# A planned order of tasks against a fixed list of all tasks, in a fused attention and feed-forward kernel

## The chip, the cores and the metric

The kernel runs on one core of one Trainium2 chip. Its time is the device time of one execution in microseconds, from the chip's own counters. The number that is predicted is the median of several executions.

A core has five engines that work side by side, each with a queue of its own that it works through in the order written: TensorE (PE, matrix products), VectorE (DVE), ScalarE (ACT), GpSimd (POOL) and SyncE (SP). Here POOL and SP mostly issue transfers. An engine waits at the head of its queue until the semaphores of that instruction allow it; what stands behind it waits too.

## The reference

```python
# attention, batch 8, heads 8, seq 576, head_dim 64
scores = scale * np.matmul(q, k.transpose(0, 1, 3, 2))
thresh = np.max(scores, axis=-1, keepdims=True) - tau
scores = np.where(scores >= thresh, scores, -1000000000.0)
scores = scores - np.max(scores, axis=-1, keepdims=True)
attn = np.exp(scores)
attn = attn / (np.sum(attn, axis=-1, keepdims=True) + 1e-09)
out = np.matmul(attn, v)
# (B,H,S,D) -> (4608, 512), then the feed-forward layer
h = x @ w_in                                # 512 -> 2048
g = h * (1.0 / (1.0 + np.exp(-1.702 * h)))
y = g @ w_out                               # 2048 -> 512
```

All in float32. The two weights are loaded once and rewritten on the chip, the feed-forward rows are taken in 18 blocks of 256 tokens.

## The kernel before

**Attention.** Two heads make a pair; there are 32 pairs, 0 to 31. A pair's scores come in nine groups of 64 keys: `scores` (L818) computes one group on TensorE as four 64x64 tiles side by side, `keep` (L835, ACT) copies it out of PSUM, `in_groups` (L858, DVE) takes maxima. After the row maximum is spread, `sub` (L940, DVE) or an accumulating transfer (`add_mb`, L933, POOL queue) takes it off, `mask` (L947) and `exps` (L951) run on ACT, and `values` (L962, TensorE, again 64x64 tiles) multiplies by v. Three PSUM places ("psA") hold scores on their way; a group of scores needs one, and `keep` frees it. From pair 6 on, the values of one pair and the scores of the next are written as one **run**: values of two groups, two groups of scores, and so on, fourteen pieces in turn. I write V12.1 for part 1 of the values of pair 12, S13.2 for group 2 of the scores of pair 13. Such a run uses TensorE in four small tiles; the feed-forward products use it whole (128x128).

**Feed-forward.** Blocks 0 and 1 use plain products (`mm1_0`, L1159, then `tanh`, L1116, on ACT and `gelu_0`, L1165, on DVE). Later blocks use seven products of half blocks in place of eight (`product1`, L1223, and `product4`, L1396, for the first layer; `product`, L1704, for the second). I write P0.0 for the first task of `product` of block 0. The last six blocks, after the last pair, use two levels of this (`product2`, L1551; `product3`, L1660); DVE and ACT do the additions and copies around them. Before the second layer can start, the 32 pieces of the weights are converted on ACT and DVE as they land (`cv_power`, `cv_power2`, `cv_whole`, `cv_end`, L746 to L771) and summed (`t_whole`, L1289).

**The order.** All work is first noted as 4767 tasks by `task(...)`, each with an engine, a cost, a rank and the tasks it comes after. `run_in_order` then plays a clock forward: at each moment an engine that is free takes, of the tasks that are ready and find their buffers free, the one with the lowest rank, and emits its instructions. A list of ranks, `PLACES`, one number for each task, sets the choice. Transfers are tasks of two movers ("DMS", "DMW") with a rate. `follows` ties the pieces of a run: once TensorE has begun a run, `held_for` keeps it from taking anything else until the next piece is ready:

```python
for rank, i in queue if engine in MOVERS else sorted(queue):
    if engine == "PE" and held_for not in (None, i):
        continue
```

and `need` lets a run begin only with all three psA places free. Forty tiny products (`stay_warm`, L1770) are tasks of the lowest rank, used while TensorE has nothing else, up to about 37 us. What is emitted is a plain program: the planner is gone when the chip runs it, and each engine's instructions stand in the order in which the planner took them.

Of the kernel before, what the change touches and what calls it, by code (L numbers as in the profile page):

```python
# [17 lines left out]
ALU = mybir.AluOpType  # L18
# [14 lines left out]
def kernel(  # L33
# [40 lines left out]
    NKT = NK // 2  # L74
# [179 lines left out]
    ALIKE = ("sub", "keep", "x_sum", "x_sum0", "x_sum3", "read", "in_groups", "cv_low", "cv_round", "place_x")  # L254
# [28 lines left out]
    def transfer(by, time, a, kind=0, give=(), lag=1.7):  # L283
# [6 lines left out]
    PLACES = """  # L290
# [2562 lines left out]
```

## Time and profile before

| what | us |
|---|---|
| median of 3 executions (1219.2 to 1220.19) | 1219.4 |
| the profiled execution's own time | 1218.41 |
| its span, first to last instruction | 1216.6 |
| PE busy in the span | 1194.1 |
| DVE busy | 1067.2 |
| ACT busy | 794.0 |
| POOL busy | 130.8 |

PE is busy 98% of the span, but that is an average over stages. A busy PE can also be one that runs tiny products to fill time, or one whose clock was halved. The profile is read by stretches of the span: which engine has no idle time in each, and what it is that PE waits for.

### The profile page before, as it was taken

The page shows a single profiled execution, that of the slowest core. Times are in us where ns is not written, and L with a number is a line of the kernel's source. Part 1 is how long each engine was busy: PE and PEld are TensorE (multiplying, and loading weights), DVE is VectorE, ACT ScalarE, POOL GpSimd, SP SyncE. Part 2 cuts the span into 40 slices and gives each one's busy share as a digit, 9 for nine tenths or more (in the row PEclk, how much of TensorE's full clock was granted, in tenths as well). Part 3 has the DMA queues.
Part 4 walks back from the last instruction along what each step waited for, and adds up shares of the span by engine and source line. Part 5 has one row for each costly group of instructions (what it writes and reads, how often), then busy time and mean ns, then how long its engine had stood idle before and what let it go on. Part 6 is the DMA issues. An engine that isn't in the chain of part 4 may idle for free.

```text
span 1216.6 us, 26169 instructions
## 1 busy us (share of the span) xinstructions
PE 1194.1 (98%) x10560; PEld 979.7 (81%) x10560; DVE 1067.2 (88%) x1622; ACT 794.0 (65%) x1183; POOL 130.8 (11%) x176
## 2 busy tenths in 40 slices
PE   8899999999999999999999999999999999999998
PEld 6556777788877777777777777777778999999998
DVE  6998998989989888999889867997896799899797
ACT  7999986888686779668876659667872340340340
POOL 0112232110001110011100110021100000000000
PEclk9999999999999999999999999999999999999999
DMA  8866769787555664567635743567623544544442
GB/s 263 225 137 157 189 146 178 138 157 198 132 131 122 143 164 93 133 145 183 142 74 123 175 108 79 123 138 179 166 59 123 183 137 142 165 135 144 141 139 94
DMA packets 220616, 176.55 MB, mean 145 GB/s; under 512 B 148752, under 2 KB 165776, under 8 KB 220368
## 3 DMA queue, kind: packets, MB, share of 16 engines
q1 hardware_dynamic: 197776, 125.42, 37.9%
q0 software_dynamic: 22032, 49.17, 20.3%
q8 instruction: 83, 1.36, 0.5%
q10 hardware_dynamic: 688, 0.30, 0.1%
q14 instruction: 37, 0.30, 0.1%
HBM read 119.53 MB, written 25.84 MB: 119 GB/s over the span
## 4 chain that ended last, share of the span: by engine, by line
PE 79%; ACT 14%; DVE 3%; issue 1%; DMA 1%; ACTq 0%; DVEq 0%
PE ops L1704 24%; PE hps L1396 9%; PE pv L962 9%; PE ps L818 9%; PE ps L1396 7%; PE ops L1660 6%; PE hps L1551 5%; PE ps L1660 4%; PE ps L1551 4%; ACT arena L835 3%; ACT arena L947 3%; ACT arena L951 3%; PE hps L1223 2%; DVE arena L1568 1%; PE ps L1223 1%
## 5 line engine op out<-in xcount | busy, mean ns | idle before, releaser
L858 DVE TRANSPOSE_TENSOR_REDUCE part<-arena 128x36 f32<-128x1152 f32 (+1 forms) x250 | 296.7, 1213 | 25.1 <-ACT arena L835 18.5
L835 ACT COPY arena<-ps 128x576 f32<-128x576 f32 x288 | 172.3, 646 | 52.3 <-PE ps L818 49.4
L947 ACT ACTIVATE arena<-arena 128x1152 f32<-128x1152 f32 (+1 forms) x160 | 167.8, 1064 | 55.2 <-DVE arena L940 53.7
L951 ACT ACTIVATE arena<-arena,shift 128x1152 f32<-128x1152 f32 (+1 forms) x160 | 183.8, 1160 | 2.4
L818 PE MATMUL ps<-arena 64*64 64x288 f32 x2304 | 173.1, 408 | 10.8 <-ACT arena L835 7.3
L1704 PE MATMUL ops<-w_out,arena 128*128 128x256 f32 x768 | 173.9, 381 | 2.7 <-DVE arena L1165 2.7
L1704 PEld LDWEIGHTS ops<-w_out,arena 128*128 128x128 f32 x768 | 144.5, 190 | 28.1 <-issue 4.4
L962 PE MATMUL pv<-arena 64*64 64x288 f32 x2176 | 159.4, 405 | 0.0
L818 PEld LDWEIGHTS ps<-arena 64*64 64x64 f32 x2304 | 81.0, 132 | 74.6 <-ACT arena L835 32.1
L940 DVE TENSOR_TENSOR arena<-arena 128x1152 f32<-128x1152 f32 (+1 forms) x100 | 130.3, 1339 | 0.8
L962 PEld LDWEIGHTS pv<-arena 64*64 64x64 f32 x2176 | 80.5, 133 | 52.4 <-issue 5.6
L1565 ACT COPY arena<-hps 128x512 f32<-128x512 f32 x66 | 38.6, 585 | 114.8 <-PE hps L1551 114.8
L1704 PE MATMUL ops<-arena 128*128 128x256 f32 x464 | 104.3, 379 | 0.0
L933 POOL DMA_DIRECT2D arena<-arena x50 | 54.3, 1321 | 422.0 <-DVE arena L898 246.2
L1704 PEld LDWEIGHTS ops<-arena 128*128 128x128 f32 x464 | 88.0, 190 | 12.8 <-issue 0.4
L848 DVE TRANSPOSE_TENSOR_REDUCE part<-arena 128x72 f32<-128x2304 f32 x25 | 64.3, 2573 | 14.7 <-ACT arena L951 14.5
L1396 PE MATMUL hps<-xT,w_in 128*128 128x256 f32 x256 | 59.0, 381 | 0.0
L1396 PEld LDWEIGHTS hps<-xT,w_in 128*128 128x128 f32 x256 | 48.1, 190 | 8.9 <-issue 2.2
L878 ACT ACTIVATE other<-red,gap 32x18 f32<-32x18 f32 x100 | 30.7, 307 | 36.9 <-DVE red L867 35.8
L1159 PE MATMUL hps<-xT,w_in 128*128 128x256 f32 x232 | 53.0, 389 | 0.0
L1437 ACT COPY arena<-hps 128x512 f32<-128x512 f32 x64 | 37.0, 578 | 24.0 <-PE hps L1396 23.9
L1568 DVE TENSOR_TENSOR arena<-ps,arena 128x512 f32<-128x512 f32 x63 | 42.8, 686 | 10.0 <-ACT arena L1565 7.6
(224 smaller groups left out, 2045.2 us busy)
## 6 DMA issues: line engine op xcount, KB each, us to landing
arena<-in_v_dram SPq DMA_DIRECT2D x128, 144.0 KB
arena<-exu SPq DMA_DIRECT2D x63, 256.0 KB
arena<-ext SPq DMA_DIRECT2D x60, 256.0 KB
arena<-arena POOLq DMA_DIRECT2D x25, 576.0 KB, 6.1
arena<-wrow POOLq DMA_DIRECT2D x48, 256.0 KB, 4.6
arena<-in_k_dram SPq DMA_DIRECT2D x112, 72.0 KB
arena<-in_q_dram SPq DMA_DIRECT2D x112, 72.0 KB
arena<-arena POOLq DMA_DIRECT2D x25, 288.0 KB, 7.3
```

The source lines that it names most:

```text
L818: nc.tensor.matmul(ps[ts(c, KT), h, 0:SH], lhsT=mats[n, 1][ts(h, D), ts(j, KT)], rhs=mats[n, 0][ts(h, D), ts(c, SH)], start=True, stop=True,)
L835: nc.scalar.copy(out=sT[n, t][:, u], in_=pss.pop((n, j))[:, :, 0:SH])
L848: nc.vector.tensor_reduce(out=stats[n, ALU.add][:, t * 2 * QB : min(2 * t + 4, NK) * QB], in_=arena2[:, lo : mid + size].rearrange("p (c d ...
L858: nc.vector.tensor_reduce(out=stats[n, op][:, t * 2 * QB : min(2 * t + 2, NK) * QB], in_=sT[n, t].rearrange("p u h (g d) -> p (u h g) d", ...
L940: engine.tensor_tensor(out=s, in0=s, in1=mbs[n].unsqueeze(1).to_broadcast(list(s.shape)), op=ALU.add if n in BY_DMA or n in NEGATED else A ...
L947: nc.scalar.activation(out=s, in_=s, func=AF.Prelu, alpha=STEEP)
L951: nc.scalar.activation(out=s, in_=s, func=AF.Exp, scale=SCALE, bias=shift)
L962: nc.tensor.matmul(o[c][ts(h, D), 0:SH], lhsT=left(j, h)[ts(c, KT)], rhs=sT[n, t][ts(c, KT), u, h, :], start=(j == 0), stop=(j == NK - 1),)
L1396: nc.tensor.matmul(o[:, ts(j, BLK)], lhsT=left[:, c, ts(j, P)], rhs=right[:, c, :], start=(x in (P1, P2, P5) and j + c == 0), stop=(j + c ...
L1551: nc.tensor.matmul(o[:, ts(j, HT)], lhsT=left[:, ts(j, P)], rhs=right, start=(m in (P1, P2, P5) and j == 0), stop=(j == 3), skip_group_che ...
L1660: nc.tensor.matmul(banks3[pos, r][:, 0:HT], lhsT=left[:, j, :], rhs=right[:, j, :], start=(m in (P1, P2, P5) and j == 0), stop=(j == 3), s ...
L1704: nc.tensor.matmul(banks[blk][k][:, ts(o, HM)], lhsT=left[:, j, :], rhs=right[:, j, :], start=(j == 0), stop=(j == HF - 1),)
```

## The change

`PLACES`, the planner's clock, the movers' rates, `need` and `follows` are gone from the emission. In their place stands `ORDER`, a list of all 4767 task numbers, and the tasks are emitted in that order:

```diff
-    PLACES = """
+    ORDER = """
...
     def run_in_order():
-        for i, place in enumerate(PLACES):
-            tasks[i] = (*tasks[i][:2], int(place), *tasks[i][3:])
...
-                    if engine == "PE" and held_for not in (None, i):
-                        continue
...
-        assert started == len(tasks), (started, len(tasks))
+        assert len(ORDER) == len(tasks)
+        for i in map(int, ORDER):
+            x_free.extend(x_used.pop(key) for key in x_ends.get(i, ()) if key in x_used)
+            tasks[i][3](*tasks[i][4])
```

The costs given to `task(...)` are changed as well (for example 1.25 to 1.136 for `t_whole`); nothing reads them any more. The functions that emit instructions are the same, and so are the tasks. So the whole change is in the order of each engine's queue. Laid beside the order that the planner gave before, the list keeps this many tasks of each engine in their old relative order (the longest common sequence):

| engine | tasks | in the old order |
|---|---|---|
| PE | 1161 | 1042 |
| DVE | 1394 | 860 |
| ACT | 1055 | 808 |
| SP | 461 | 330 |
| POOL | 133 | 126 |

No task goes far: most are exchanged with neighbours. After 200 us the order on PE differs in few places until the last pair is done. These are the places on PE, with the tasks in question in brackets (the last line is one engine's neighbours on DVE and ACT):

```
block 0   before: mm1_0 13, [V5 whole], mm1_0 14, mm1_0 15, P0.0
          after:  mm1_0 13, mm1_0 14, mm1_0 15, [V5 whole], P0.0
run 6/7   before: V6.3 S7.6 S7.7 V6.4 S7.8 [P0.3 first half]
          after:  V6.3 S7.6 S7.7 [P0.3 first half] V6.4 S7.8
run 12/13 before: [P3.0 j0-3] V12.0 S13.0 S13.1 V12.1 S13.2 S13.3 V12.2 S13.4 ... S13.8 [P3.0 j4-6]
          after:  V12.0 S13.0 S13.1 V12.1 [P3.0 j0-3] S13.2 S13.3 V12.2 [P3.0 j4-6] S13.4 ... S13.8
run 19/20 before: [product4 6.0.3] V19.0 ... S20.3 V19.2 S20.4 ...
          after:  V19.0 ... S20.3 V19.2 [product4 6.0.3] S20.4 ...
run 25/26 before: V25.3 S26.6 S26.7 V25.4 S26.8 [P8.0 j7]
          after:  V25.3 [P8.0 j7] S26.6 S26.7 V25.4 S26.8
pair 31   before: [V31 whole], last product of block 10, first of block 11
          after:  last product of block 10, first of block 11, [V31 whole]
DVE       before: t_whole x4, sub 6.0, [sub 6.1, sub 6.2], gelu_0 14, gelu_0 15
          after:  t_whole x4, sub 6.0, gelu_0 14, gelu_0 15, ... [sub 6.1] ... [sub 6.2]
ACT, 19   before: exps 19.0, mask 19.1, mask 19.2, [keep4], exps 19.1, [keep4], exps 19.2, [keep4], mask 19.3, keep 20.0
          after:  exps 19.0, mask 19.1, exps 19.1, mask 19.2, exps 19.2, mask 19.3, keep 20.0, keep 20.1, [keep4]
```

In the first 40 us the list loads the second piece of the weights ahead of the q of pair 1, and the v of pair 0 five weight pieces later; the 40 `stay_warm` tasks are spread differently. In the last 265 us (`product2`, `product3`) many neighbours are exchanged on PE, DVE and ACT; the last four tasks of PE and the last two of DVE are the same.

More of the change, by code (lines that the diff above doesn't have):

```diff
@@ L253 @@
     AGAIN, COLD = {"DVE": 0.12, "ACT": 0.13}, 0.1
-    ALIKE = ("sub", "keep", "x_sum", "x_sum0", "x_sum3", "read", "in_groups", "cv_low", "cv_round", "place_x")
+    ALIKE = ("silu1", "silu4", "t_whole", "t_minus", "sub", "keep", "x_sum", "x_sum0", "x_sum3", "read", "in_groups", "cv_low", "cv_round", "place_x")
     ENTER = {True: 0.0, False: 0.22}
@@ L1829 @@
         ]
-        m = task("ACT", 0.75, rank, cv_power, i, after=[a] + over)
-        m = task("ACT", 0.56, rank, cv_power2, i, after=[m])
+        m = task("ACT", 0.667, rank, cv_power, i, after=[a] + over)
+        m = task("ACT", 0.62, rank, cv_power2, i, after=[m])
         if i in ROUND_BY_ACT:
@@ L1834 @@
         else:
-            a = task("DVE", 0.35, rank, cv_whole, i, after=[a])
-        ready_w.append(task("DVE", 0.61, rank, cv_end, i, after=[a, m], give=place))
+            a = task("DVE", 0.332, rank, cv_whole, i, after=[a])
+        ready_w.append(task("DVE", 0.602, rank, cv_end, i, after=[a, m], give=place))
     warm = task("ACT", 2.3, -2.0, first_act)
@@ L1891, in first_blocks @@
             a = task("ACT", 0.48, FIRST, tanh, j, after=ffn[-1:], take=("io",) + (("xT",) if j == 0 else ()))
-            gelus[j] = task("DVE", 0.59, FIRST, gelu_0, j, after=[a],
+            gelus[j] = task("DVE", 0.6, FIRST, gelu_0, j, after=[a],
                 give=("psM", "io"),
@@ L1899, in t_sum @@
                 for k in range(2):
-                    after = [task("DVE", 1.25, T_RANK, t_whole, x, k, after=after)]
+                    after = [task("DVE", 1.136, T_RANK, t_whole, x, k, after=after)]
                 t_ready.extend(after)
@@ L2309, in seven @@
         ):
-            last = task("ACT", 0.93, FIRST, silu1, f, h, after=after + [last])
+            last = task("ACT", 0.95, FIRST, silu1, f, h, after=after + [last])
             gs[f, h] = [last, last]
@@ L2387, in seven4 @@
                         keeps[x, y] = task(
[L2388 removed]
+                            "ACT", 0.466, FIRST, keep4, q, x, after=ffn[-1:], give=("psM",) if x == P4 else (),
                         )
@@ L2474, in alone @@
         ):
-            last = task("ACT", 0.93, FIRST, silu1, f, h, after=after + [last])
+            last = task("ACT", 0.95, FIRST, silu1, f, h, after=after + [last])
             gs[f, h] = [last, last]
@@ L2566, in valued @@
         placed[n] = task(
-            "DVE", 0.9, float(n), place_x, n, after=[summed[n], pv], take=("xT",) * len(new),
+            "DVE", 0.857, float(n), place_x, n, after=[summed[n], pv], take=("xT",) * len(new),
             give=("psA", rc_pool(n)),
@@ L2641 @@
             )
-            pq = task("ACT", 0.56, r, turned, n, 0, after=[pq], take=own(n, "qkT0"), give=("psA",))
-            pk = task("DVE", 0.66, r, turned, n, 1, after=[pk], take=own(n, "qkT1"), give=("psA",))
+            pq = task("ACT", 0.52, r, turned, n, 0, after=[pq], take=own(n, "qkT0"), give=("psA",))
+            pk = task("DVE", 0.668, r, turned, n, 1, after=[pk], take=own(n, "qkT1"), give=("psA",))
         else:
-            pq = pk = task("DVE", 1.26, r, prep, n, after=lq + lk, take=("qkT0", "qkT1"), give=("raw0", "raw1"))
+            pq = pk = task("DVE", 1.288, r, prep, n, after=lq + lk, take=("qkT0", "qkT1"), give=("raw0", "raw1"))
         preps.append([pq, pk])
@@ L2727 @@
         else:
-            m = task("DVE", 0.78, r, spread_max, n, after=[a], take=own(n, "mb"))
+            m = task("DVE", 0.702, r, spread_max, n, after=[a], take=own(n, "mb"))
         spread.setdefault(n, m)
@@ L2786 @@
                     su = [a]
-                a = task("DVE", 1.07, r, one_row, n, after=[a], give=("psA",))
+                a = task("DVE", 0.95, r, one_row, n, after=[a], give=("psA",))
         if n not in SUMS_BY_PE:
             if n >= SINGLE:
-                su = [task("DVE", 1.28, r, in_groups, n, 0, ALU.add, after=ws[:1])]
+                su = [task("DVE", 1.292, r, in_groups, n, 0, ALU.add, after=ws[:1])]
                 for t in PAIRED:
@@ L2793 @@
                 su += [
-                    task("DVE", 0.77 if t == NKT else 1.28, r, in_groups, n, t, ALU.add, after=[ws[t]])
+                    task("DVE", 0.66 if t == NKT else 1.292, r, in_groups, n, t, ALU.add, after=[ws[t]])
                     for t in range(len(su), NKT + 1)
@@ L2798 @@
                 su = [
-                    task("DVE", 0.77 if t == NKT else 1.28, r, in_groups, n, t, ALU.add, after=[ws[t]])
+                    task("DVE", 0.66 if t == NKT else 1.292, r, in_groups, n, t, ALU.add, after=[ws[t]])
                     for t in range(NKT + 1)
@@ L2814 @@
         if n not in SUMS_BY_DMA:
-            summed[n] = task("DVE", 1.15, r, spread_sums, n, after=[a], take=(rc_pool(n),))
+            summed[n] = task("DVE", 0.98, r, spread_sums, n, after=[a], take=(rc_pool(n),))
         if pv is not None:
```

179 lines of the change are left out of this document (42 added, 137 removed), and 383 rows, old and new, of tables (ORDER, PLACES).

## The prediction

> **What bounds the kernel now.** The span first, then busy time by stretches, then the waits of the engine that is full in each stretch, then the chain and the timeline at those waits.
>
> The page's head, and a view of busy time by stretches whose bounds I set where the bound changes (columns: stretch, its length, then busy time and instruction count of PE, PE's weight loads, DVE, ACT, POOL; granted clock; share of the DMA engines; GB/s):
>
> ```profile
> span 1216.6 us, 26169 instructions
> PE 1194.1 (98%) x10560; PEld 979.7 (81%) x10560; DVE 1067.2 (88%) x1622; ACT 794.0 (65%) x1183; POOL 130.8 (11%) x176
> ...
> 9.40:106.20 96.80, 87.97 (x1254) 51.07 (x1247) 88.92 (x138) 95.92 (x140) 17.63 (x24) 0.99 0.80 208
> 106.20:107.70 1.50, 1.50 (x8) 0.76 (x10) 0.75 (x2) 0.05 (x1) 0.22 (x1) 0.51 0.92 147
> 107.70:163.00 55.30, 53.52 (x368) 42.01 (x368) 53.70 (x77) 54.77 (x81) 12.86 (x20) 1.00 0.71 168
> 163.00:177.60 14.60, 11.94 (x107) 8.71 (x105) 13.33 (x20) 10.21 (x14) 5.50 (x7) 1.00 0.57 122
> 177.60:350.00 172.40, 172.40 (x1603) 140.32 (x1604) 156.51 (x205) 130.21 (x185) 25.12 (x26) 1.00 0.77 163
> ...
> 949.70:1213.00 263.30, 263.07 (x2353) 262.69 (x2351) 237.17 (x521) 78.34 (x157) 0.00 (x0) 1.00 0.48 145
> 1213.00:1216.60 3.60, 0.00 (x0) 0.00 (x0) 0.25 (x1) 0.00 (x0) 0.00 (x0) 1.00 0.19 60
> ```
>
> The reader is to see two stages. From 9.4 to 163 us ACT is full: 95.92 of 96.80, then (after a hole of 1.45 in 1.50) 54.77 of 55.30. PE is not; it has the tiny filler products in its busy time too. From 163 us PE takes over and is full to the end: all of 177.6 to 350, and 263.07 of 263.30 in the last stage. The 3.6 us at the end are the last addition and stores.
>
> So only two kinds of idle time are worth money: ACT's before 163, PE's after it. The view of waits gives both; first ACT's in 0 to 163, then PE's in 163 to 178 and, two rows, in 177.6 to 949.7 (columns: engine and line, waited for whom, total, times, longest):
>
> ```profile
> ACT arena L808 <- PE ps L796: 3.9, 1, 3.9
> ACT arena L835 <- PE ps L818: 2.3, 2, 2.1
> ACT xT L1116 <- PE hps L1159: 1.5, 1, 1.5
> ...
> ACT w_out L746 <- DMA arena<-in_moe_w_out_dram: 1.7, 1, 1.7
> ...
> PE ps L818 <- ACT arena L835: 3.4, 4, 1.2
> PE ops L1704 <- DVE arena L1165: 2.7, 1, 2.7
> ```
>
> After 163 us PE idles 2.7 us once (ahead of the first product of the second layer, waiting for the last `gelu_0`) and 3.4 us in four waits inside runs, where the next group of scores waits for `keep` to free a psA place. That is all: 6.1 us.
>
> **The change part by part.** No instruction is added or removed, so the cost is only in who waits. My base is the profiled execution, 1218.41 us (span 1216.6 and 1.8 around it); the median is 1.0 above it, and I add that at the end.
>
> 1. *The values of pair 5 go behind the last two plain products.* The chain of waits before the change at this place, and the timeline's rows of the DVE additions behind it:
>
> ```profile
> 160.71 5.55 DMA arena<-in_moe_w_out_dram
> ...
> 167.34 1.20 DVE w_out L771 x2
> 168.54 2.27 DVE w_out L1289 x2
> ...
> 171.86 1.22 DVE arena L1289
> 173.08 2.50 DVE arena L940 x2
> ...
> 176.80 0.69 DVE arena L1165
> 177.54 10.63 PE ops L1704 x48
> ```
>
> Before, PE's last plain product ends near 174.8 (177.54 less the wait of 2.7); `gelu_0` 15 needs it and ends at 177.5. In the list V5 stands behind these products, 4.5 us by the row of V31 below (the same 72 records), so they end near 170.3 and PE can be at P0.0 with no hole, at 174.8. But DVE must be too: it ends `t_whole` at 173.08, since that hangs on the last weight piece (landed 166.26). Then the list has one `sub` and two `gelu_0` where before stood three `sub` (two of them left behind): 1.25 + 2 x 0.69 from the rows gives 175.7. Gain 177.5 - 175.7 = 1.8; the whole 2.7 if the piece lands a little sooner, 0 if it lands 2 us later. I take 1.8. What is late next: V6, which needs all five `exps` of pair 6. ACT has one unit more ahead of it now, but its idle time around 163 to 168 (the 1.7 in the row above) gives room; I cost this at nothing, and at up to 1.2 (one `exps`, the row below) if that room is not there.
>
> ```profile
> 919.12 4.53 PE pv L962 x72
> ...
> L951 ACT ACTIVATE arena<-arena,shift 128x1152 f32<-128x1152 f32 (+1 forms) x160 | 183.8, 1160 | 2.4
> ```
>
> 2. *Runs interrupted.* PE's timeline in the run 12/13 with its two waits, ACT's in the same window, and the chain in the run 19/20:
>
> ```profile
> 360.74 1.26 PE L818 MATMUL ps<-arena 64*64 64x288 f32 x16 [0.70 <-ACT arena L835]
> ...
> 364.16 1.26 PE L818 MATMUL ps<-arena 64*64 64x288 f32 x16 [1.19 <-ACT arena L835]
> ...
> 353.60 3.99 ACT L1248 ACTIVATE arena<-arena 128x1024 f32<-128x1024 f32 x4
> 357.61 1.28 ACT L951 ACT_TABLE_LOAD   x1
> ...
> 551.78 0.59 ACT arena L1437
> ...
> 553.52 0.57 ACT arena L1437
> ...
> 559.84 0.66 issue
> 560.50 0.63 ACT arena L835
> ```
>
> In run 12/13 PE idles 0.70 and 1.19, since ACT is held up by four `silu1` (3.99) and a table load (1.28). The list does not move ACT's `silu1` out of the way, so ACT sets the end of this run as before. Of the two products put into the waits one stood ahead of the run (its hour is only moved), the other behind it: that one is gained. Its length: 3/4 of a full product task.
>
> ```profile
> 396.58 3.65 PE ops L1704 x16
> 400.23 3.45 PE hps L1396 x16
> ```
>
> Sixteen records are two tasks of four matmuls and take 3.45, so three matmuls take 1.3. The same two rows give the price of turning from small tiles to the whole array: 3.65 against 3.45, 0.2 us each time. Here it falls into ACT's waiting time. Gain 1.3, between 0 and 1.9 (all the wait).
>
> In run 19/20 PE waits 1.0 us of the 3.4. The product put in stood ahead of the run, so by itself it gains nothing; but the list also takes three `keep4` (0.59 and 0.57 in the rows) from ahead of the `exps` and `keep` for which PE waits, 1.7 us in all. So ACT is there before PE is. Gain 1.0, between 0 and 1.0. In run 25/26 the rest of the 3.4, 0.5 us: one matmul (0.43) comes from behind into the wait. Gain 0.4. In run 6/7 PE had no wait; the interruption costs one turn, 0.2, and gains nothing unless V6.4 is late now. Loss 0.2.
>
> 3. *ACT and DVE before 163 us.* The first 221 ACT tasks, up to the last `tanh`, are the same tasks in both orders; only their sequence differs. ACT is full there, so this stage cannot shrink by more than its hole of 1.45, and each us for which the list makes ACT wait is added to the total. I take 0, with -1.5 and some +8 as ends (rivals).
>
> 4. *SP and POOL.* The list puts the second weight piece ahead of the q of pair 1:
>
> ```profile
> GB/s 263 225 137 157 189 146 178 138 157 198 132 131 122 143 164 93 133 145 183 142 74 123 175 108 79 123 138 179 166 59 123 183 137 142 165 135 144 141 139 94
> ...
> w_out<-in_moe_w_in_dram SPq DMA_DIRECT2D x12, 511.8 KB
> ```
>
> One piece at 263 GB/s is 1.9 us, by which pair 1's q is later; before, no ACT row waits for it (the only row on L808 is the first, 3.9), and the list turns it in one group of scores later (0.5 us). Between 0 and 1.4; I take 0, as ACT has `keep` 0.6 to do meanwhile. The v of pair 0 goes behind five more pieces, some 10 us, hidden by the whole softmax of that pair, ahead of which it isn't used; without that cover PE would wait, but PE is not the full engine there. POOL moves seven tasks, busy 11%, hidden by its own idle time.
>
> 5. *The last stage.* PE is busy 263.07 of 263.30, so the exchanges there can gain 0.2 at most. DVE is busy 237.17 of 263.3, 90%, so an exchange that is wrong by one addition costs 0.3 to 0.7 once. I take 0.
>
> Sum: -1.8 - 1.3 - 1.0 - 0.4 + 0.2 = -4.3. 1218.4 - 4.3 = 1214.1; with the 1.0 to the median **1215.1**.
>
> **The rivals.**
>
> *ACT stalls early: slower.* The planner emitted what was ready by its clock; the list need not. One place decides: ACT's queue before 163 us, where a conversion (`cv_power`) that stands ahead of a `keep` waits for its piece and everything behind waits too. For: 247 ACT tasks are out of place; the second piece's conversion is the 12th ACT task and was the 16th; DMA is busy 0.80 there. Against: the loads were moved with them. Price: a wait on a landing is 1.7 us in the one row that there is; five such are 8.4, which gives 1215.1 + 8.4 = **1223.5**. It decides from 4.3 us of new idle time on.
>
> *Nothing gained.* ACT and DVE set the end of the runs and of the start of the second layer, and PE's waits only move to the next group. For: in run 12/13 ACT is full, and three of the four waits are ends of ACT chains. Then only the matmul of 0.4 stays against 0.2: **1219.2**.
>
> *The clock hole goes: faster still.* PE's timeline and the stretch at 104 us:
>
> ```profile
> 102.89 1.20 PE L818 MATMUL ps<-arena 64*64 64x288 f32 x16 [1.80 <-DVE xT L1073]
> 104.02 3.60 PE L1159 MATMUL hps<-xT,w_in 128*128 128x256 f32 x8
> ...
> 104.00:107.70 3.70, 3.70 (x16) 2.50 (x16) 2.65 (x5) 2.21 (x5) 2.42 (x3) 0.54 1.01 178
> ```
>
> After a wait of 1.80 the clock is half (0.54) for 3.4 us: eight records take 3.60, which is 1.9 more than half of the 3.45 that sixteen take above, and ACT's `tanh` waits 1.5 for them (the row above). If the new order keeps PE busier ahead of this, the 1.5 is gained: **1213.6**. Against: the same wait for `place_x` of pair 3 is in the list, with the same scores around it. [...]
>
> **How the numbers follow.** Forecast, 1215.1: 0.50; from 1213.5 (all 6.1 less the 0.2) to 1217.8 (part 1 alone). Clock hole gone, 1213.6: 0.14. Nothing gained: 0.13. ACT stalls: 0.23. About 0.2%, 2.4 us, is what a measurement of this kernel can tell from no change: 1217.0 to 1221.8. Faster: 0.14, and 0.47 of the forecast's 0.50, is 0.61. Same: 0.13 and the forecast's 0.03, 0.16. Slower: 0.23. The range goes from 1211.0 (both the forecast's best and the clock hole, less 1) to 1223.0, which leaves out half of the ACT stalls (0.12) and 0.05 below.
>
> **What would show it.** Right: PE's row "ops L1704 <- DVE arena L1165" falls from 2.7 to under 1; PE's row "ps L818 <- ACT arena L835" falls from 3.4 to under 1; the first product of the second layer starts near 175.7 and PE stays full after it. Part 3 holds if ACT's hole in 9.4 to 163 stays near 2 us. Wrong: ACT waits on `in_moe_w_in` or `in_moe_w_out` landings before 163 us, or new PE waits behind 177 us that lie on DVE, or a second stretch of half clock.

## The result, and the profile after

The kernel after takes 1211.8 us (median of four executions, 1211.2 to 1213.7), the kernel before 1219.3 beside it; the ratio is 0.9942, with an interval from 0.9925 to 0.996. The forecast was 1215.1, faster by 4.2; the kernel gained 7.5. The profiled execution took 1211.57 us, of which 1209.5 are its span. One execution of all those told below, of the list with its runs whole, took 2513 us, about twice the time, and is left out of every number.

The page's head, and busy time by stretches of the profile after (same columns as before):

```profile
span 1209.5 us, 26132 instructions
PE 1192.7 (99%) x10560; PEld 980.6 (81%) x10560; DVE 1062.4 (88%) x1622; ACT 790.0 (65%) x1183; POOL 131.3 (11%) x176
```

```profile
9.40:104.00 94.60, 85.54 (x1245) 51.58 (x1243) 87.74 (x141) 93.90 (x140) 16.87 (x24) 1.00 0.85 204
104.00:159.00 55.00, 53.42 (x369) 41.65 (x369) 53.77 (x80) 54.53 (x83) 12.96 (x20) 1.00 0.78 183
159.00:172.60 13.60, 13.31 (x113) 9.81 (x111) 11.82 (x18) 8.87 (x14) 5.83 (x8) 1.00 0.58 125
172.60:350.00 177.40, 176.71 (x1641) 144.26 (x1639) 160.29 (x206) 135.56 (x191) 26.03 (x27) 1.00 0.77 161
350.00:944.00 594.00, 593.67 (x4735) 464.49 (x4734) 512.68 (x653) 417.74 (x600) 67.81 (x86) 1.00 0.55 130
944.00:1206.00 262.00, 262.00 (x2343) 261.77 (x2342) 234.18 (x526) 76.88 (x157) 0.00 (x0) 1.00 0.47 144
```

The lines of the kernel have moved up: `scores` is L818 before, L733 here and L718 in most of the experiments; `keep` is L835, L750 and L735, `product` L1704, L1619 and L1604.

The two stages are still there: ACT is full to 159 us, PE from 159 on. The stretch of half clock at 104 us is gone (every row has 1.00), and the hole ahead of the second layer has shrunk: in 159 to 172.6 PE is busy 13.31 of 13.60, where it was busy 11.94 of 14.60. The waits of PE from 172 us on, then those of ACT up to 163 us:

```profile
PE ops L1619 <- DVE osb L1641: 0.7, 1, 0.7
PE ps L733 <- DVE arena L1158: 0.2, 1, 0.2
```

```profile
ACT arena L723 <- PE ps L711: 4.0, 1, 4.0
ACT w_out L661 <- DMA arena<-in_moe_w_out_dram: 2.7, 1, 2.7
ACT arena L750 <- PE ps L733: 2.4, 2, 2.1
```

The two rows that carried the forecast (2.7 for `gelu_0`, 3.4 for `keep`) are gone; 0.9 is left, in two new rows that wait for DVE. The chain of waits of the kernel after, where the first layer of block 0 ends:

```profile
156.29 6.02 DMA arena<-in_moe_w_out_dram
...
163.02 0.59 ACT xT L1031
...
163.63 0.70 DVE arena L1080
...
164.37 3.72 PE hps L1074 x16
168.09 4.53 PE pv L877 x72
172.62 10.56 PE ops L1619 x48
```

In this profile the last weight piece still stands in the chain, but by another way. In the list `cv_power` 31 stands ahead of `tanh` 13, so `tanh` waits for the landing, and behind it come the plain products, V5 and P0.0 with no hole.

To say where the 7.05 us of the two profiles lie, I take the starts of the same tasks from the timelines. The last two columns are runs told below: the list a second time, and the planner's order without half clock.

| from the start of ... to the start of ... | before | after | list again | planner, waits filled |
|---|---|---|---|---|
| span's start, first transposition | 5.45 | 4.91 | 5.41 | 5.81 |
| to `mm1_0` 0 | 98.57 | 97.73 | 99.20 | 99.67 |
| to `mm1_0` 2 | 5.68 | 4.04 | 4.04 | 4.04 |
| to P0.0 | 67.84 | 65.87 | 65.17 | 67.74 |
| to V7.0 | 38.66 | 39.96 | 39.33 | 38.66 |
| to V28.0 | 614.73 | 612.02 | 612.02 | 614.73 |
| to the first `product2` | 118.66 | 118.30 | 118.30 | 118.65 |
| to the end | 266.97 | 266.68 | 266.57 | 267.45 |
| sum, the span | 1216.56 | 1209.51 | 1210.04 | 1216.75 |

The third line is the half clock, 1.64. The fourth and sixth are the forecast's parts 1 and 2. The fifth is a loss. The last two are small gains, 0.36 and 0.29, that I had put at 0.

The first two lines mix two things. In three profiles, the last two columns and one more, the first record of full clock lies some 4 us later (at 8.9 to 9.8 us in place of 3.7 to 5.6) and the first values of pair 0 start 1.5 to 1.7 us later (the last section has more). Among the profiles that begin alike, `mm1_0` 0 starts 103.8 to 104.6 us behind the span's start in the six whose start is in the planner's order, and 102.6 to 103.4 in the four with the list's start: 1.1 us earlier on average. So the list gains about 1 us here, in a stage that I had put at 0. ACT's time up to there, before and after:

```profile
9.40:104.00 94.60, 85.77 (x1248) 49.33 (x1240) 87.03 (x135) 93.75 (x137) 15.43 (x23) 1.00 0.80 208
```

```profile
9.40:102.60 93.20, 84.14 (x1239) 50.34 (x1236) 86.34 (x140) 92.50 (x137) 15.47 (x22) 1.00 0.85 204
```

ACT is full in both, and as many instructions (137) take 93.75 before and 92.50 in the list. Why they take less is told below, with the price of ACT's order.

### The profile page after: what moved, and what is told of

Read it like the earlier page. It is cut to its first block, busy times and chain, and to the rows that moved or that the text cites. A ratio compares the mean times of both kernels' runs of the same rounds, so it can differ in the third digit from the quotient of the medians.

```text
span 1209.5 us, 26132 instructions
## 1 busy us (share of the span) xinstructions
PE 1192.7 (99%) x10560; PEld 980.6 (81%) x10560; DVE 1062.4 (88%) x1622; ACT 790.0 (65%) x1183; POOL 131.3 (11%) x176
## 4 chain that ended last, share of the span: by engine, by line
PE 85%; ACT 8%; DVE 3%; DMA 2%; issue 1%; ACTq 0%; POOL 0%; SPq 0%; DVEq 0%
PE ops L1619 23%; PE pv L877 10%; PE ps L733 9%; PE hps L1311 9%; PE ps L1311 7%; PE ops L1575 6%; PE hps L1466 6%; PE ps L1575 5%; PE ps L1466 5%; PE hps L1138 2%; ACT arena L750 2%; PE ps L1138 2%; ACT arena L866 2%; ACT arena L862 2%; DMA arena<-in_moe_w_out_dram 1%; ACT w_in L661 1%
## 5 line engine op out<-in xcount | busy, mean ns | idle before, releaser
L750 ACT COPY arena<-ps 128x576 f32<-128x576 f32 x288 | 172.2, 646 | 61.5 <-PE ps L733 60.1
L866 ACT ACTIVATE arena<-arena,shift 128x1152 f32<-128x1152 f32 (+1 forms) x160 | 183.1, 1161 | 2.1
L733 PE MATMUL ps<-arena 64*64 64x288 f32 x2304 | 173.3, 407 | 6.0 <-ACT arena L750 2.9
L1619 PE MATMUL ops<-w_out,arena 128*128 128x256 f32 x768 | 174.8, 382 | 0.7 <-DVE osb L1641 0.7
L1619 PEld LDWEIGHTS ops<-w_out,arena 128*128 128x128 f32 x768 | 144.1, 190 | 28.1 <-issue 7.5
L733 PEld LDWEIGHTS ps<-arena 64*64 64x64 f32 x2304 | 82.2, 132 | 66.3 <-ACT arena L750 23.7
L1480 ACT COPY arena<-hps 128x512 f32<-128x512 f32 x66 | 38.2, 585 | 121.1 <-PE hps L1466 116.5
L1619 PE MATMUL ops<-arena 128*128 128x256 f32 x464 | 104.3, 379 | 0.0
L1619 PEld LDWEIGHTS ops<-arena 128*128 128x128 f32 x464 | 88.0, 190 | 12.8 <-issue 0.9
L1311 PEld LDWEIGHTS hps<-xT,w_in 128*128 128x128 f32 x256 | 48.0, 190 | 9.4 <-issue 2.6
L1074 PEld LDWEIGHTS hps<-xT,w_in 128*128 128x128 f32 x232 | 43.4, 190 | 10.4 <-DVE arena L1080 3.3
```

The source lines that it names most:

```text
L733: nc.tensor.matmul(ps[ts(c, KT), h, 0:SH], lhsT=mats[n, 1][ts(h, D), ts(j, KT)], rhs=mats[n, 0][ts(h, D), ts(c, SH)], start=True, stop=True,)
L750: nc.scalar.copy(out=sT[n, t][:, u], in_=pss.pop((n, j))[:, :, 0:SH])
L866: nc.scalar.activation(out=s, in_=s, func=AF.Exp, scale=SCALE, bias=shift)
L1074: nc.tensor.matmul(hidden[j][:, ts(i, BLK)], lhsT=w_in[:, c, ts(j, P)], rhs=xTs[i][:, c, :], start=(c == 0), stop=(c == NDC - 1), skip_gro ...
L1311: nc.tensor.matmul(o[:, ts(j, BLK)], lhsT=left[:, c, ts(j, P)], rhs=right[:, c, :], start=(x in (P1, P2, P5) and j + c == 0), stop=(j + c ...
L1619: nc.tensor.matmul(banks[blk][k][:, ts(o, HM)], lhsT=left[:, j, :], rhs=right[:, j, :], start=(j == 0), stop=(j == HF - 1),)
```

## The experiments

All are the kernel after with another list (the planner's order is such a list too, and gives the kernel before). "Planner's" below means that order. Ratios are to the kernel before, with 95% intervals, from 5 rounds.

**The start alone and the rest alone.** Two lists cut at P0.0:

```diff
-ORDER = list
+ORDER = planner's order of the tasks that the list has ahead of P0.0, then the list   # old start
+ORDER = list up to P0.0, then the planner's order of the others                        # old rest
```

> The planner's order for every task that the list has ahead of the first product of the second layer (P0.0), the list's order from there on. The prediction's terms: only the runs count here (-1.3 -1.0 -0.4 +0.2), so 2.5 us under the kernel before, about 1216.8. The theory from the two traces, that most of the gain is made ahead of P0.0: 1.7 under it, 1217.6, and P0.0 starts at 177.5 as before.

> The list's order up to P0.0, the planner's order from there on. The prediction's terms: 1.8 under the kernel before, 1217.5. The theory from the traces: 5.0 under it, 1214.3, with P0.0 at 172.5 and PE's waits of 3.4 in the runs as before.

Old start: 1213.7 us, ratio 0.9955 (0.994 to 0.997). Old rest: 1215.5, 0.9961 (0.9948 to 0.9973). Each half gains, and neither as was expected of it: old start is 5.0 under the kernel before, where 2.5 or 1.7 was expected, old rest 3.2, where 1.8 or 5.0 was. Old start reaches P0.0 as early as the list does (65.62 us behind `mm1_0` 2, against 67.84 before and 65.87 after), though V5 stands where it stood. So the list's order of ACT and DVE ahead of 163 us is not what moves P0.0 against `mm1_0` 2. Of the tasks that DVE had to do ahead of `gelu_0` 14 and 15, only `sub` 6.1 and 6.2 have changed sides: they are behind P0.0 in the list, hence behind `gelu_0` here. Old rest is early at P0.0 too (65.81) and then loses 4.0 against the list, 1040.9 from P0.0 to the end against 1037.0.

**The two moves of part 1, and the interrupted runs, in the planner's order.**

```diff
 # PE, first kernel
-mm1_0 13, V5, mm1_0 14, mm1_0 15, P0.0
+mm1_0 13, mm1_0 14, mm1_0 15, V5, P0.0
 # DVE, first kernel
-sub 6.1, sub 6.2, gelu_0 14, gelu_0 15
+gelu_0 14, gelu_0 15, sub 6.1, sub 6.2
 # PE, second kernel (with the keep4 of run 19/20 as in the list)
-[P3.0 j0-3] V12.0 ... V12.1 S13.2 ... V12.2 S13.4 ... S13.8 [P3.0 j4-6]
+V12.0 ... V12.1 [P3.0 j0-3] S13.2 ... V12.2 [P3.0 j4-6] S13.4 ... S13.8
 ...                                        # 19/20 and 25/26 as in the list
```

> The planner's order with one move: the values of pair 5 behind the last two plain products, and sub 6.1 and 6.2 behind the last gelu_0. The prediction's part 1: P0.0 at 175.7, 1.8 us under the kernel before, 1217.5. The rival: nothing (1219.3), because what holds P0.0 is the landing of the last weight piece at 166.3 and what hangs on it.

> The planner's order with the three interrupted runs alone (12/13, 19/20 with the three keep4 behind the exps, 25/26). The prediction's part 2: -1.3 -1.0 -0.4, so 2.7 us under the kernel before, 1216.6, and PE's waits on keep in the runs go from 3.4 to under 1. The rival that the waits only move: 0.4 under it, 1218.9, and the 3.4 stay.

The moves of part 1 gave 1219.3, ratio 1.0001 (0.9988 to 1.0014): nothing, as the rival had it, but not for its reason, since P0.0 does come 1.39 earlier (66.45) and what follows comes later. The runs gave 1218.1, 0.9991 (0.9977 to 1.0005). By the median that is inside the noise; by the trace it is clear. The waits of PE behind 177 us, before 3.4 in four, in the kernel with the runs interrupted:

```profile
PE ps L718 <- ACT arena L735: 0.5, 1, 0.5
```

and from V7.0 to the end it takes 998.3 us, where the planner's order takes 1000.4 and 1000.8 (its two profiles): 2.1 to 2.6 gained, of the 2.7 that I gave the three runs.

The medians hide this because the clock differs from execution to execution, and each execution's granted clock is on record. Of the 30 of the kernel before, 13 had a full clock (1.000), with a mean time of 1217.5. All twelve with the moves of part 1 had it, with a mean of 1219.0, and three with the runs interrupted, with a mean of 1214.6. At equal clock the moves of part 1 lose 1.6 and the runs gain 2.9.

**The two `sub` alone.** The trace of the kernel before says that V5 need not move for P0.0 to come early; this leaves it.

```diff
 # DVE; nothing else moves
-sub 6.1, sub 6.2, gelu_0 14, gelu_0 15
+gelu_0 14, gelu_0 15, sub 6.1, sub 6.2
```

> The planner's order, with one exchange alone: sub 6.1 and sub 6.2 behind gelu_0 14 and 15 on DVE; V5 stays where it was. Exchange theory: P0.0 starts 2.0 to 2.5 us earlier against the start of the scores than in a run of the planner's order without half clock, but V6.0 waits for exps of pair 6 and gives 2 us or more back: median as before's within 0.7 us. The prediction's part 1: moving V5 is what lets P0.0 come early, so without it P0.0 gains nothing. If the gain at P0.0 stays: median 1.8 below before's.

1218.8 us, 0.9997 (0.9984 to 1.001). P0.0 does start early, 64.99 behind `mm1_0` 2, as early as in the list. But V6.0 then starts 14.55 behind P0.0 in place of 10.56. The wait of PE, the stretch behind it, and ACT's timeline:

```profile
PE ops L1604 <- ACT osb L1619: 2.2, 1, 2.2
```

```profile
183.90:187.30 3.40, 3.35 (x8) 2.73 (x9) 3.40 (x4) 3.37 (x4) 0.45 (x1) 0.50 0.82 119
```

```profile
175.36 1.73 ACT L847 ACTIVATE arena<-arena 128x576 f32<-128x576 f32 x2
178.76 1.16 ACT L847 ACTIVATE arena<-arena 128x1152 f32<-128x1152 f32 x1 [1.67 <-DVE arena L840]
...
183.53 0.36 ACT L1619 ACTIVATE osb<-ops 128x256 f32<-128x256 f32 x1
```

ACT's queue still has `mask` 6.2 right behind `mask` 6.0. Its `sub` is late now, so ACT stands 1.67 us, and the `read` of the first product (183.53), for which PE waits, is the fifth task behind it. On top of that came half a clock (0.50) for the 3.4 us behind the wait.

**Both queues.** So the gain should hold if ACT's order behind P0.0 changes with DVE's.

```diff
 # DVE, from gelu_0 to turn_sums 6, in the list's order
-sub 6.1, sub 6.2, gelu_0 14, gelu_0 15, place_x 5, s_sums, s_minus, ...
+gelu_0 14, gelu_0 15, place_x 5, sub 6.1, s_sums, s_minus, s_second, sub 6.2, ...
 # ACT, from the last tanh to keep 7.3, in the list's order
-mask 6.0, mask 6.2, exps 6.4, t_minus x2, exps 6.0, read, exps 6.2, mask 6.1, exps 6.1, ... cross_sums 6, keep 7.0
+exps 6.4, mask 6.0, t_minus x2, mask 6.1, read, exps 6.0, w_copy, exps 6.1, mask 6.2, exps 6.2, ... keep 7.0-7.3, cross_sums 6
```

> The planner's order on TensorE, SP and POOL without any exchange (V5 stays ahead of the last plain products, the runs stay whole). Only two stretches of two queues, between the last tanh and S7.3, take the list's order: on DVE sub 6.1 and sub 6.2 go behind gelu_0 15 and the additions behind them follow the list; on ACT mask 6.2 goes behind exps 6.1, mask 6.0 behind exps 6.4, cross_sums 6 behind the first keep of pair 7. Two-queue theory: P0.0 comes 2.4 us earlier as with the two sub alone, and since ACT no longer stands at mask 6.2, V6.0 starts 10.6 us behind P0.0 again (with the two sub alone it was 14.5, of which 2.2 one wait and 1.7 half clock): median 2.4 us below before's, ratio 0.998. Rival (what keeps the early P0.0 from being given back is the rest of the list, its earlier exps or its interrupted runs): median as before's within 0.7 us.

V6.0 is back at 10.56 behind P0.0, as expected. The median is not: 1218.3, 0.9993 (0.9981 to 1.0006), where 0.998 was expected. The next run gives the rest back. PE's timeline in run 7/8:

```profile
217.69 1.26 PE L718 MATMUL ps<-arena 64*64 64x288 f32 x16 [1.25 <-ACT arena L735]
```

From V7.0 to V9.0 it takes 53.1 us, in the planner's order and in the list 51.5: 1.6 lost. So my second theory, that the two queues up to S7.3 are all that part 1 needs, fell as well. In the five kernels that have the early P0.0 and the planner's order further on (old rest, the moves of part 1 and the four places below among them), V6.0 and V9.0 together come 1.6 to 4.0 us late; in the five with the list's order behind P0.0, as in "old start", neither does. Which exchange behind P0.0 does it is not shown.

**Four places together**, the kernel before with these two queues and the three runs:

> The kernel of both queues with the three runs 12/13, 19/20 and 25/26 interrupted as well (keep4 of run 19/20 moved as in the list): four places of the order changed, everything else the planner's. If these four places are the whole gain that isn't clock: profile 2.4 + 2.1 = 4.5 us below one of the planner's order without half clock (1215.1 less 4.5: span 1210.6), median at most 1.5 us above the list's. Rival (the early stage of the list has a share of its own): median 2 us or more above the list's.

1215.6, ratio 0.9972 (0.9958 to 0.9986), 3.6 us above the list run beside it. The expectation fails and the rival's condition is met. The rival's reason holds for about 1 us of it: `mm1_0` 0 starts at 103.9, as in the planner's order. From `mm1_0` 2 to P0.0 it takes no longer than the list (65.06 against 65.17). The larger part of what is missing lies later: 614.2 from V7.0 to V28.0 against the list's 612.0 (run 7/8 again), and 385.7 against 384.9 from there to the end. It takes 2.25 less from V7.0 to the end than the kernel with both queues alone: the runs once more.

**The list with its runs whole again.**

```diff
 # PE (and the neighbours of run 19/20 on ACT, DVE, SP in the planner's order)
-V12.0 ... V12.1 [P3.0 j0-3] S13.2 ... V12.2 [P3.0 j4-6] S13.4 ... S13.8
+[P3.0 j0-3] V12.0 ... V12.1 S13.2 ... V12.2 S13.4 ... S13.8 [P3.0 j4-6]
 ...
```

> The list, with the runs 12/13, 19/20 and 25/26 whole again (the products back ahead of or behind them, the three keep4 of run 19/20 back in the planner's places). Runs theory: P0.0 stays at 172.5, the time from P0.0 to the end grows by 2.1 us, and PE's waits for keep inside the runs come back with 3 us: median 1213.9. Rival (the list's other exchanges on ACT and DVE have made the interruptions needless): waits for keep stay under 1 us, median 1211.8 as the list's.

The waits of PE are back:

```profile
PE ps L718 <- ACT arena L735: 3.5, 4, 1.2
```

and from V7.0 to the end it takes 999.4 us against the list's 997.0: 2.4 lost. The median is 1215.5, ratio 0.9966 (0.9953 to 0.9979); by the ratios that is 2.9 to 3.4 above the list's, which the intervals do not tell apart from the 2.4. P0.0 stays as early as expected (65.12), so the rival is out.

**The clock.** Between 60 and 180 us PE has two waits of more than 1.5 us in the planner's order: 1.8, behind S5.2, and 2.7, ahead of P0.0. In the profile before the first is followed by half a clock. Tiny products now fill both; nothing reads their results.

```diff
+    def fill(times, d):
+        for r in times * (0, 1):
+            nc.tensor.matmul(
+                d[ts(r, KT), r, SH : SH + P], lhsT=ones[ts(r, KT)], rhs=eye[ts(r, KT)],
+                start=True, stop=True,
+            )
...
+            if i == 607:     # P0.0
+                fill(9, psA.tile([P, 2, 512], FP32, name="ps", tag="ps"))
             tasks[i][3](*tasks[i][4])
+            if i == 752:     # S5.2
+                fill(6, pss[5, 2])
```

> The planner's order, with TensorE's two waits ahead of 180 us (1.8 us behind S5.2, 2.7 us ahead of P0.0) filled with tiny products whose results nothing reads; 12 and 18 records of the kind that takes 0.065 us each. No task is moved. Clock theory: these two waits are why the clock halves in the kernel before, in some executions or all; filled, there is no half-clock stretch, the profile is 1.5 us shorter than before's (1215.1), the median 1.0 to 1.5 below that of before, and the single times lie closer together than before's 1215.9 to 1223.2. Rival (the half clock is an accident of one profile and no part of the median's gain): the median as before's within 0.5 us, the spread as wide.

The stretches at the first wait and at the half clock, before (the second is shown in the prediction) and filled:

```profile
99.50:103.50 4.00, 2.19 (x40) 1.09 (x36) 3.90 (x11) 3.96 (x7) 3.12 (x6) 1.00 0.55 113
```

```profile
99.50:103.50 4.00, 4.00 (x70) 2.80 (x70) 3.33 (x10) 3.96 (x8) 1.62 (x3) 1.00 0.47 90
104.00:107.70 3.70, 3.35 (x29) 2.25 (x33) 3.40 (x6) 3.70 (x7) 2.08 (x4) 1.00 0.63 176
```

PE goes from 2.19 busy in 4.00 to full, and the clock stays at 1.00 (0.54 before). The median is 1216.7 against 1220.0 for the kernel before beside it; the ratio is 0.9985 (0.9971 to 0.9999). The twelve times lie between 1215.9 and 1219.3, the 29 of before between 1216.0 and 1222.8: the lowest is the same, the high ones are gone. No task was moved and work was added, so the planner's order owed about 2 us of its median to these two waits (1.8 by the ratio, 3.3 by the medians; the interval allows 0.1 to 3.5). The profile itself was expected to be 1.5 shorter and was not, since it began late (below); from `mm1_0` 0 on it takes 1.3 less than before.

The granted clocks say the same without any change to the kernel. The profile before has one half-clock stretch, of 3.41 us (104.24 to 107.66), in a span of 1216.6, which lowers the mean clock by 0.0014, and its mean is 0.999; by the same sum I estimate that 0.997 is two. The 81 executions of the kernel before that stand beside the experiments:

| granted clock | executions | mean time, us |
|---|---|---|
| 1.000 | 28 | 1217.3 |
| 0.999 | 32 | 1219.5 |
| 0.998 to 0.996 | 21 | 1221.6 |

The rows are 2.2 and 2.1 apart, and ordered by clock the middle execution is in the second. All twelve executions of the filled kernel are at 1.000 or 0.999, and its five at 0.999 are no slower than its seven at 1.000 (1216.9 against 1217.4).

Half a clock followed the wait at 100 us in the profile before, but not in all: the kernel with the runs interrupted and "old start" have the same wait at 100 us and no half clock in their profiles. Which of the two waits does most was not tried apart, but the executions give a hint. Where both waits stand (before, runs interrupted) 31 of 93 executions have a full clock; where the second has gone or shrunk to 1.0 or less and the first stands (five kernels) 42 of 53 have it.

The half-clock stretch of the kernel before lasts 3.413 us in the trace, and in three profiles the distance ahead of the half clock is a whole multiple of that. From the first record of full clock to the half clock it is 98.99 us before, 174.08 in "the two `sub` alone" and 51.20 in the list again, which is 29, 51 and 15 times 3.413, and the first record lies between 3.7 and 9.8 us behind the span's start. What sets these steps is not shown. Counted in them, PE is busy for 0.37 to 0.47 of the step ahead of each of the five half-clock stretches in the profiles (before: 1.60 of 3.41 us from 100.83 on); but steps of 0.43 to 0.47 also pass without one in seven profiles (the list's first: 1.50 of 3.41 from 55.86 on), so this share alone does not decide.

**The price of ACT's order.** In the traces before and after a `mask` that is followed at once by its own `exps`, or a `cv_power` by its own `cv_power2`, delays it by 0.12 to 0.16 against another neighbour. By the gaps in the traces the planner's order has 14 such neighbours among ACT's first 221 instructions and the list 2; up to `mm1_0` 0 it is 8 and none. That fits the 1.25 us that ACT's instructions take less there. Here the list gets 58 more.

```diff
 # ACT ahead of 160 us, 29 times each
-mask, X, exps                  cv_power, X, cv_power2
+X, mask, exps                  X, cv_power, cv_power2
```

> The list, with 58 tasks of ACT ahead of 160 us moved down to right ahead of the one that needs them: 29 mask to ahead of their exps, 29 cv_power to ahead of their cv_power2. In the traces so far a task takes 0.13 to 0.15 us longer there when it stands right behind the one it needs; so 58 x 0.14 = 8.1 us more for ACT. ACT theory (ACT sets the end of the start): less the 2.7 us that ACT waits for the last piece of the weights in the list, P0.0 and the end come 5.4 us later: median 1217.2. Rival (DVE and the last weight piece set it, and the list's gain in ACT's time is no part of the result): P0.0 and the median within 1 us of the list's, 1211.8 to 1212.8.

1230.9 us, ratio 1.0101 (1.008 to 1.0122): 19 above the list. P0.0 starts at 188.5, 15.9 later. Stretches that end with the same task of ACT (the last `exps` of pair 5), list and this kernel:

```profile
9.40:157.90 148.50, 137.86 (x1608) 92.26 (x1606) 140.41 (x219) 147.34 (x219) 28.73 (x41) 1.00 0.82 196
```

```profile
9.40:174.00 164.60, 139.67 (x1609) 94.40 (x1602) 141.39 (x219) 154.52 (x219) 30.26 (x42) 0.99 0.73 181
```

ACT's 219 instructions take 7.2 longer (8.1 was expected), 0.12 for each of the 58. ACT also idles 8.9 more, which was not expected: the median should have been 1217.2. So ACT does set the end of the start, and its 7.2 came out doubled. That the other 8.9 follow from the longer instructions alone is argued and not shown, since the exchange also puts 58 tasks later, and DVE and PE get their results later.

**The list mended, and the list again.**

```diff
 # ACT                          # DVE                               # PE, run 6/7
-cv_power 31, tanh 13           -cv_whole 31, gelu_0 13             -S7.7 [P0.3 first half] V6.4 S7.8
+tanh 13, cv_power 31           +gelu_0 13, cv_whole 31             +S7.7 V6.4 S7.8 [P0.3 first half]
                                -sub 6.0, gelu_0 14, gelu_0 15
                                +gelu_0 14, gelu_0 15, sub 6.0
```

> The list with three exchanges more. tanh 13 goes ahead of the last weight piece's cv_power 31 on ACT and gelu_0 13 ahead of its cv_whole 31 on DVE (in the list both stand behind a landing for which ACT waits 2.7 us); sub 6.0 goes behind gelu_0 15; run 6/7 is whole again. If the last weight piece stands only before t_whole: P0.0 1.1 us earlier, and V7.0 0.7 us closer to V6.0: median 1.9 us below the list's. Rival (sub 6.0 late makes exps 6.0 and the values of pair 6 late; run 6/7's wait goes elsewhere): as the list within 0.5 us.

> The list unchanged, beside the three others on one chip: 1211.8 as before, its single times within 1211.2 to 1213.7, narrower than those of the kernel before (1215.9 to 1222.8). If the list has as many half-clock stretches as the planner's order, its times spread as widely.

The list again: 1212.0, ratio 0.9938 (0.992 to 0.9956), times from 1211.0 to 1213.1. Mended: 1210.8, 0.9933 (0.9914 to 0.9952), from 1209.9 to 1212.5. The intervals overlap, so that it beats the list is likely and not shown; 1.9 was expected, and the medians differ by 1.2. ACT no longer waits for the last piece (2.7 in the list's profile after, 0.9 in the list again), but P0.0 is not earlier (65.07 against 65.17, where 1.1 was expected): in the chain PE is full.

```profile
157.41 10.63 PE hps L1059 x48
168.03 4.53 PE pv L862 x72
172.56 2.57 PE ops L1604 x11
```

With PE full, V5's 4.53 us stand in that chain. From P0.0 to V7.0 it takes 38.66 against 39.33. Of these 0.67, 0.34 lie in run 6/7 itself (5.63 in place of 5.97 from S7.7 to the end of P0.3); the rest lies behind it, where the later `sub` 6.0 could play a part too.

The list's own times spread little, as expected, but not because it is free of half clock: six of its nine executions (four beside the kernel before, five here) have a clock of 0.999 or 0.998. Their mean is 1212.3, against 1211.3 for the three with a full clock.

## Why the prediction was right, and where it was not

**Part 1, 1.8 forecast.** P0.0 came 1.97 earlier (67.84 to 65.87; 65.0 to 66.5 in eight other kernels with the exchange of DVE, the one with ACT's 58 neighbours aside). The size was right, the reason half wrong. The prediction has V5 behind the plain products let PE come early and DVE's exchange as a second condition. The exchange does it without V5 ("the two `sub` alone"), and V5 moved with it gave no more. What failed is the sentence on what is late next, "I cost this at nothing", with ACT's idle time around 163 to 168 as cover. That idle time is no cover: `mask` 6.2 stands in ACT's queue behind the last `tanh`, and waits there for `sub` 6.2 (to 178.76 in the row above), long after 168. Alone the exchange gives back all it gained (a wait of 2.2, and 1.7 of half clock behind it), and with ACT's queue mended up to S7.3 it gives back 1.6 in run 7/8. In the list it isn't given back, since the order of ACT and DVE behind P0.0 changes as well; my zero was right by luck, for a reason that I hadn't seen.

**Part 2, 1.3 + 1.0 + 0.4 forecast for the three runs.** Measured 2.1 to 2.6 in three pairs of kernels that differ in these runs (planner's order, list, and the four places against the two queues). This is the step that held best. Run 6/7 was under-priced: 0.2 forecast, 0.34 measured in the run itself and 0.67 up to V7.0. In the profile after it is 1.30 up to V7.0, where PE also waits 0.7 for DVE's `read` (the copy of a product out of PSUM), the larger of the two new rows among its waits.

**Part 3, 0 forecast.** This step failed in its mechanism, though it cost the forecast little. "The same tasks in both orders" does not mean the same time: up to `mm1_0` 0 ACT's instructions take 1.25 less in the list, since no `exps` or `cv_power2` stands right behind the task whose result it needs, and `mm1_0` 0 starts about 1.1 earlier. ACT's waits ahead of 159 us are as before, but for the 1.5 for `tanh`, which went with the half clock. Its one wait for a landing is 2.7 in place of 1.7. That is the rival "ACT stalls early" with one landing where it needs five. That rival's ground was real: 58 exchanges of neighbours were enough for 19 us.

**Part 4** held: the wait on the row of `turned` (ACT's copy of a turned q, L808) is 4.0, before 3.9. **Part 5** nearly did: "0.2 at most" for the last stage, measured 0.29, and 0.40 in the list again; but the planner's order of this stage takes 266.7 to 267.4 from profile to profile, so that is hardly more than noise. Ahead of it lies 0.36 that I gave no term: not where V31 was moved, but in the runs 29/30 (0.10) and 30/31 (0.26), ahead of a group of scores; why was not tried.

**The clock** was a rival with a price of 1.5 and a chance of 0.14. It was 1.64 in the profile and some 2 in the median. The prediction quoted the wait of 1.80 behind which the clock was half (0.54) and then argued that the same wait was in the list. That step failed too. In the list the wait is cut up, into one of 0.48 and shorter ones, and PE is busy for 3.37 of the 4.00 us that end 0.5 ahead of `mm1_0` 0, where it was 2.19:

```profile
101.12 0.72 PE L733 MATMUL ps<-arena 64*64 64x288 f32 x8 [0.48 <-ACT arena L750]
```

The wait of 2.7 ahead of P0.0 is gone as well; the counts above hint that half a clock followed it in many executions. The list has a stretch of half clock elsewhere, at 60 us, where ACT is the bound; its second profile and the mended list show it:

```profile
60.00:64.00 4.00, 4.00 (x44) 2.31 (x44) 4.00 (x5) 4.00 (x6) 0.00 (x0) 0.57 0.74 169
```

The span of the second profile is only 0.5 longer than the other's, and the mended list with the same stretch reaches `mm1_0` 0 at 103.4, so there it costs at most a few tenths.

In sum the forecast's terms come to 4.3. In the two profiles they are 1.97 (to P0.0), 2.71 (V7.0 to V28.0) and 0.65 (behind it) gained and 1.30 lost: 4.0. With the list's second profile they are 2.67, 2.71, 0.76 and 0.67 lost: 5.5. The order's part was forecast well, by errors that cancel: run 6/7's loss was put too low, and the gains behind V28.0 had no term. What the forecast left out is the clock's 2 and about 1 in ACT's start. With them the terms come to 7.0 by the first profile and 8.5 by the second; 7.5 was measured. The medians say the same: the planner's order with its waits filled takes 1216.7, the list 1211.8 and 1212.0, which leaves 4.7 to 4.9 for the order (5.2 to 5.7 by the ratios).

Of the signs named: both rows of waits went, and PE is full behind P0.0, as forecast. P0.0 starts at 172.6, not "near 175.7": the clock's 1.6 and a start that is 1.4 earlier are in it. ACT's hole up to 163 is 3.9 (0.70 and 0.47 in the first two stretches, and 2.7), not "near 2". It cost little, since PE was nearly full by then: PE waits 0.28 ahead of the last plain product in the chain. Of the signs of being wrong two showed in small, ACT's 2.7 for a landing and PE's 0.9 for DVE.

## What to carry to other kernels

An exchange that lets one engine start early is worth what the queues behind it keep: follow the task that was moved back to the next engine that waits for it, and through the next wait, before booking the gain. Tiny products in two short waits of TensorE, 1.8 and 2.7 us, took about 2 us off the median here (1.8 by the ratio), and half a clock followed the first wait in one profile and not in two others; compare executions of equal granted clock, and the spread of the single times as well as their middle. Where ACT was full, the same instructions in another order did not take the same time: 58 more that stood right behind the one whose result they need made ACT's work 7.2 us longer (0.12 each). There it pays to put something between the two.

## What the hardware showed that I had not expected

**Dependent neighbours on ACT.** In the kernel with both queues a `mask` of 1.15 us is followed by another task after 1.05, and by its own `exps` after 1.19:

```profile
178.47 1.15 ACT L847 ACTIVATE arena<-arena 128x1152 f32<-128x1152 f32 x1
179.52 0.36 ACT L1619 ACTIVATE osb<-ops 128x256 f32<-128x256 f32 x1
...
183.02 1.15 ACT L847 ACTIVATE arena<-arena 128x1152 f32<-128x1152 f32 x1
184.21 1.26 ACT L851 ACTIVATE arena<-arena,shift 128x1152 f32<-128x1152 f32 x1
```

In these rows the `mask` and the task that does not need its result overlap by 0.10; its own `exps` starts 0.04 behind its end.

**The first microseconds.** The same 76 transpositions of q and k took 2.43 us in the profile before and 3.36 in that of the filled one, whose order is the same there:

```profile
6.28 2.43 PE L796 MATMUL ps<-eye,arena 64*64 64x64 f32 x76 [0.20 <-DMA arena<-in_q_dram]
```

```profile
6.83 3.36 PE L700 MATMUL ps<-eye,arena 64*64 64x64 f32 x76
```

In the three profiles that begin like the second (the filled one, "the two `sub` alone", the list again) the first values of pair 0 start 1.5 to 1.7 us later: at 38.78 and 38.91 against 37.32 before, and at 37.37 against 35.71 in the list's first profile. Up to 0.5 of that lies ahead of the first transposition; the rest lies in the transpositions: from the first of them to the first scores it is 3.19 us before (5.45 to 8.64) and 4.31 in the filled one (5.81 to 10.12). The views print 1.00 where the trace has no clock record, and its first record, of full clock, begins at 5.26 us before and at 8.91 in the filled one, 9.24 and 9.78 in the other two. The transpositions take 3.36 to 3.88 in these three; in the other eleven profiles, where the first record lies at 3.7 to 5.6 us, they take 2.43 to 2.62. What the clock was ahead of its first record the trace does not say, so that it made the transpositions slower is not shown. So a single profile of this kernel is uncertain by over a us from its start alone, and half clock behind a wait adds its 1.6: two spans say less than the stretches between the same tasks.
